# Three batch buffers, loads by head pairs, weights from iteration 13 on, and a feed-forward part with moving weights

## The chip, the cores and the metric

One core of one Trainium2 chip runs the kernel. The metric is the device time of one execution in microseconds (us), as the median of several runs; lower is better.

## What is computed

Two stages. The first is a linear attention with decay, over 4 batches, 8 heads, 768 steps and head size 48; the second a soft mixture of 8 experts over the 3072 rows that the first one makes.

```python
# attention: r, k, v are (4, 8, 768, 48), w and u are (8, 48), all f32
for t in range(S):
    cur = np.einsum('bhd,bhe->bhde', u[None] * kt, vt)
    y[:, :, t] = np.einsum('bhd,bhde->bhe', rt, state + cur)
    state = w[None, :, :, None] * state + np.einsum('bhd,bhe->bhde', kt, vt)
x = y as (3072, 384)                      # rows are (batch, step)
# experts: phi (384, 32), w1 (8, 384, 1024), w2 (8, 1024, 384); 4 slots per expert
logits = x @ phi
d = softmax of logits over the 3072 rows; slot_input = d.T @ x      # (32, 384)
for e in range(E):
    h = np.maximum(slot_input[e] @ w1[e], 0.0)
    slot_out[e] = h @ w2[e]
c = softmax of logits over the 32 slots; out = c @ slot_out         # (3072, 384)
```

## The kernel before, in words

**Units of work.** Two heads make a pair (96 columns), so a batch has 4 pairs and the kernel 16, numbered m. The 768 steps of a pair are two groups g of 3 chunks of 128 steps; an iteration i of the main loop (L420, i from -5 to 31) is one group of one pair, software-pipelined: at iteration i the engines finish group i (`y_pe`), form the masked attention matrix of group i+1 (`a_pe`, `mask_f`), bring v of group i+2 into step order (`v_pe`) and transpose k or r of a later pair (`t_pe`). Everything is emitted in the order of the code and each engine works through its own queue in that order.

**One pair.** GpSimd scales k and r with powers of w (`scale`, L196, into one of three buffers `kr`), from f32 tables W that VectorE multiplies and ScalarE exponentiates, one table for each pair index of a batch (`table`, L164 and L166). TensorE transposes them into the banks T0 and T1 (L203), ScalarE copies them out as kT and rT (L209), TensorE transposes kT back (L215), VectorE copies that out as kn (L220) and multiplies prod (L225). For each group: `a_pe` (L264), 64-row matmuls on the two halves of the array in turn; the mask AT on VectorE (L269), which is used here as the milestone of an iteration; `m_pe` (L279 to L294) for the state; `z_evac` on VectorE (L304 to L310); `y_pe` (L320 to L333); `y_evac` on ScalarE into x (L340).

**Routing.** From iteration 8 on, `route` adds for the groups that are finished: transposes of x (L355), logits (L348), their exponentials Lexp (L369), the sums over rows (`disp`, L386, into the same bank Mb that `m_pe` uses, accumulated in `acc`, L393), and the transposed exponentials LexpT (L375, L379). The last groups are routed after the loop (L466 to L492), up to `uns` (L498), the slots' inputs.

**Loads.** SyncE issues a batch as three DMAs of 1152 KB (k, r, v; L105, L109) into one of two buffers `raw`. Batches 0 and 1 are issued at the start, batch 2 at iteration 2 and batch 3 at iteration 10, into buffers that batches 0 and 1 have used up (L457, L459). w comes as one DMA that writes its row to all 128 partitions (L99), and with u a second time as `wu` from ScalarE's queue (L101, L102) for a transpose (L178) that yields `wuT`, `ucol` and `wT`. GpSimd's queue carries the expert weights, cast from f32 to bf16 on the way: one DMA for each of the 16 matrices, w1 of the 8 experts, then w2, spread over the iterations from -1 to 22 by the table `W_AT` (L418). w2 of the last four experts lies in `raw[0]`.

**Feed-forward and output** (L501 to L548). The weights are the stationary operand: 192 matmuls of 128x128 weights with 4 moving columns for w1 (L507), relu on ScalarE (L510), 24 row sums of LexpT (L512), another 192 for w2 (L522), copies to `soT` (L524), 3 transposes (L527), a copy to `so` (L528). Then 24 matmuls of 384 columns (L542) from six banks, which VectorE and ScalarE in turn scale and copy out (L544, L546), and 7 stores (L548).

## Time and profile before

| what | value |
|---|---|
| median of 3 runs | 164.96 us (164.61 to 164.97) |
| the profiled execution's own time | 164.48 us |
| its span, first to last instruction | 162.7 us |
| mean granted TensorE clock | 0.832 |
| PE, PEld busy | 112.8 us (69%), 92.7 us (57%) |
| DVE (VectorE), ACT (ScalarE), POOL (GpSimd) busy | 97.9 us (60%), 85.0 us (52%), 57.7 us (35%) |
| HBM read, written | 39.57 MB, 4.72 MB |

The profile shows one execution. PE is TensorE's matmuls and PEld its weight loads, which run beside them; SP is SyncE, which here only issues DMAs. A line of a group or a timeline names the source line, the engine, the operation, what it writes and reads (out<-in), the shape and the count. Ahead of an instruction stands in brackets how long its engine had been idle and what released it. The granted clock is the share of full speed at which TensorE was allowed to run. A busy engine need not be what the end waits for: the chain of waits, followed back from the last instruction, shows that.

### The profile page before, as it was taken

The numbers are of one execution on the slowest core, as the hardware profiler recorded it, in microseconds if no ns is written. First come the engines' busy times: TensorE is split into PE (matmuls) and PEld (weight loads), VectorE is DVE, ScalarE is ACT, GpSimd is POOL, SyncE is SP. The second block draws the span as 40 slices with busy tenths as digits, with TensorE's granted clock in tenths as the row PEclk, the third lists the DMA queues.
The fourth block names the chain that finished last, engine by engine and source line by source line (L and its number), as shares of the span: only waits on it lengthen the run. The fifth ranks groups of instructions, "written<-read, shape, count | busy, mean of one in ns | idle before, by whom it ended". The sixth has DMA issues, their size and how long they took to land. (4 is left out here: it accounts for less than half of the span.)

```text
span 162.7 us, 4640 instructions
## 1 busy us (share of the span) xinstructions
PE 112.8 (69%) x1964; PEld 92.7 (57%) x1964; DVE 97.9 (60%) x202; ACT 85.0 (52%) x173; POOL 57.7 (35%) x61
## 2 busy tenths in 40 slices
PE   0023597688889760495997889599597799976840
PEld 0013395476778650385876678487486599962310
DVE  4421589999999951099399469569864300225650
ACT  3413957658777610795576398177355411005550
POOL 5053474799924007996009992000000000000000
PEclk9999999999999998589599699879959755555555
DMA  4999999599999999999999999950000000002996
GB/s 66 314 377 352 385 312 181 115 225 282 225 231 236 232 283 359 376 222 231 223 224 267 210 213 213 214 114 0 6 0 0 4 4 0 4 4 97 387 420 257
DMA packets 21500, 32.00 MB, mean 197 GB/s; under 512 B 1000, under 2 KB 17512, under 8 KB 21480
## 3 DMA queue, kind: packets, MB, share of 16 engines
q0 software_dynamic: 3328, 12.58, 38.9%
q1 hardware_dynamic: 18128, 19.12, 35.6%
q8 instruction: 15, 0.25, 0.6%
q14 instruction: 5, 0.04, 0.1%
q10 hardware_dynamic: 24, 0.00, 0.0%
HBM read 39.57 MB, written 4.72 MB: 272 GB/s over the span
## 5 line engine op out<-in xcount | busy, mean ns | idle before, releaser
L196 POOL TENSOR_TENSOR kr<-raw,W 128x576 bf16<-128x576 f32 x32 | 44.6, 1409 | 34.3 <-DMA raw<-in_r_dram 11.6
L269 DVE TENSOR_TENSOR AT<-Ab,mask_ut 128x768 bf16<-128x768 f32 x32 | 30.4, 951 | 6.5 <-PE Ab L264 6.5
L203 PE MATMUL T<-ident,kr 128*128 128x128 bf16 x192 | 18.6, 242 | 5.7 <-POOL kr L196 5.7
L209 ACT COPY kT<-T 128x768 bf16<-128x768 bf16 x16 | 12.8, 803 | 18.2 <-PE T L203 18.2
L249 PEld LDWEIGHTS <-Q 128*128 128x128 bf16 x288 | 17.7, 106 | 5.4 <-issue 4.2
L249 PE MATMUL Vb<-v_bf,Q 128*128 128x96 bf16 x288 | 19.5, 219 | 1.6 <-ACT v_bf L234 1.6
L220 DVE COPY kn<-T 128x768 bf16<-128x768 bf16 x16 | 8.9, 554 | 14.7 <-PE T L215 14.5
L203 PEld LDWEIGHTS <-kr 128*128 128x128 bf16 x192 | 13.6, 109 | 6.2 <-POOL kr L196 6.2
L225 DVE TENSOR_TENSOR prod<-T,kT 128x768 bf16<-128x768 bf16 x16 | 15.2, 949 | 1.6 <-ACT rT L209 1.6
L340 ACT CAST x<-Yb 128x288 bf16<-128x288 f32 x32 | 12.8, 399 | 5.6 <-PE Yb L333 5.0
L209 ACT COPY rT<-T 128x768 bf16<-128x768 bf16 x16 | 12.8, 799 | 5.0 <-PE T L203 3.4
L310 DVE TENSOR_TENSOR dv<-vn,Mb 128x288 bf16<-128x288 bf16 x32 | 14.2, 445 | 0.0
L234 ACT CAST v_bf<-raw 128x1152 bf16<-128x1152 f32 x8 | 9.2, 1154 | 8.3 <-DMA raw<-in_v_dram 8.3
L255 ACT CAST vn<-Vb 128x288 bf16<-128x288 f32 x32 | 12.9, 402 | 1.1 <-PE Vb L249 0.5
L264 PE MATMUL Ab<-rT,kT 64*128 64x128 bf16 x192 | 11.9, 235 | 1.9 <-DVE AT L269 1.8
L331 PE MATMUL Yb<-Z,rT 128*128 128x96 bf16 x80 | 10.5, 217 | 2.7 <-DVE Z L308 2.7
L290 PE MATMUL Mb<-vn,kn 128*128 128x96 bf16 (+2 forms) x80 | 12.3, 256 | 0.0
L308 DVE TENSOR_TENSOR Z<-Mb,bmask 128x192 bf16<-128x192 f32 x32 | 11.1, 348 | 0.0
L320 PE MATMUL Yb<-vn,AT 128*128 128x48 bf16 x192 | 10.9, 191 | 0.0
L333 PE MATMUL Yb<-dv,ident 128*128 128x288 bf16 x32 | 10.0, 311 | 1.3
L386 PE MATMUL Mb<-Lexp,x 128*128 128x32 bf16 x72 | 3.3, 180 | 9.5 <-DVE dv L310 8.6
L320 PEld LDWEIGHTS <-AT 128*128 128x128 bf16 x192 | 7.4, 100 | 3.7 <-issue 1.0
(119 smaller groups left out, 209.4 us busy)
## 6 DMA issues: line engine op xcount, KB each, us to landing
w_all<-in_moe_w_dram POOLq DMA_DIRECT2D x8, 768.0 KB, 9.7
raw<-in_k_dram SPq DMA_DIRECT2D x4, 1152.0 KB, 12.3
raw<-in_r_dram SPq DMA_DIRECT2D x4, 1152.0 KB, 10.7
raw<-in_v_dram SPq DMA_DIRECT2D x4, 1152.0 KB, 19.9
w_own<-in_moe_w_dram POOLq DMA_DIRECT2D x4, 768.0 KB, 11.2
raw<-in_moe_w_dram POOLq DMA_DIRECT2D x4, 768.0 KB, 13.1
out_dram<-raw SPq DMA_DIRECT2D x3, 768.0 KB, 3.3
out_dram<-W SPq DMA_DIRECT2D x2, 768.0 KB, 3.7
```

The source lines that it names most:

```text
L196: O(pool.tensor_mul(kr[:, j].rearrange("p j (h s) -> p j h s", s=64)[:, :, :, 0:D], src, W[j][:, q].rearrange("p j (h d) -> p j h d", h=2)))
L203: O(pe.transpose(bank[:, x * C:(x + 1) * C], kr[:, j, x, :], ident[:]))
L209: O(act.copy(t[:].rearrange("p (s j) -> p s j", j=J), bank[:, 0:S].rearrange("p (j s) -> p s j", j=J)))
L225: O(dve.tensor_mul(pr[:].rearrange("p (s j) -> p s j", j=J), T1[:, 0:S].rearrange("p (j s) -> p s j", j=J), st["kT", m][:].rearrange("p (s ...
L249: O(pe.matmul(Vb[:, c * P2:(c + 1) * P2], Q3[:, o:o + C], vb[:, 2 * q:2 * q + 2, j, :], start=(j == 0), stop=(j == JV - 1)))
L255: O(act.copy(vn[:].rearrange("p c e d -> p (c e d)"), Vb[:, 0:L * P2]))
L264: O(pe.matmul(Ab[:, e, c * C:(c + 1) * C], kT[s, t], rT[s, t]))
L269: O(dve.tensor_mul(AT[:], Ab[:, :, 0:T].rearrange("p e (c t) -> p e c t", c=L), mask_ut[:, None, None, :].to_broadcast([128, 2, L, C])))
L290: O(pe.matmul(o, kn[:, g * L + c, :], vc, start=first, stop=True, skip_group_check=True))
L310: O(dve.tensor_mul(dv[:], st["v", i][:].rearrange("p c e d -> p (c e) d"), Mb[:, 288:288 + 2 * L, None].to_broadcast([128, L * 2, D])))
L320: O(pe.matmul(Yb[:, o:o + D], AT[:, e, c, :], vn[:, c, e, :], start=first, stop=False, skip_group_check=True))
L340: O(act.copy(st["x", n][:, :, q * P2:(q + 1) * P2], Yb[:, 0:L * P2].rearrange("p (c e) -> p c e", c=L)))
```

## The change

- **Buffers.** Three `raw` buffers instead of two, so batch 2 has its own and its loads follow batches 0 and 1 at once; batch 3 reuses `raw[0]` from iteration 3 on. `w2_own` is gone: w2 of experts 0 to 3 lies in `raw[1]`, of experts 4 to 7 in `raw[2]`, and the output buffers in `raw[0]`.
- **Loads by pairs.** Batches 0 and 1 come in four pieces of two heads, k, r, v each (24 DMAs of a quarter's size); batches 2 and 3 whole. v is cast once a pair (576 columns a partition) instead of once a group of a batch (1152).
- **Weights.** `W_AT` issues them from iteration 13 to 28, the last one after the loop in two halves. w2 is read in longer rows.
- **Start.** w comes as one row to one partition and is spread by an f32 matmul of 384 columns; TensorE gets 5 dummy matmuls of 512 columns ahead of it and 7 before the loop (`keep_warm`). The first pair is scaled by VectorE instead of GpSimd; memsets move from VectorE to GpSimd; the tables are made in the middle of an iteration, one iteration later.
- **Feed-forward.** The slots' inputs are the stationary operand (32 columns, of which the 4 of one expert and zeros), the weights move: 48 matmuls of 512 columns for w1, 64 of 384 for w2. The four experts of a half write to PSUM partitions 0, 32, 64 and 96, that is, to four column strips of the array. h is transposed in between (16 transposes, two copies of 1024). In w2's first half (experts 0 to 3) the four strips alternate; in the second half each expert's 8 matmuls follow one another. Lexp, LexpT and `so` are laid out over 128 partitions for it, with zeros between.
- **Small moves.** `phi_s` is cast in three pieces, at iteration 4; `le_t` and `let_ev` of group 5 stand ahead of the last transposes.

On VectorE at the start, ahead of the loop's first instructions: W_124 and W_125 (before), W_153 and W_154 (after) are the tables for k and r, kr the scaled pair. Before:

```order
L156 CAST ident<-ident_f 128x128 [waits Pool_49]
L164 TENSOR_TENSOR W_124<-w_rep,sk 128x576 [waits Activation_49]
L164 TENSOR_TENSOR W_125<-w_rep,sr 128x576 [waits DVE_49]
L171 MEMSET bmask 128x96
L172 MEMSET bmask 64x48 [waits DVE_49]
L173 MEMSET bmask 64x48
L175 MEMSET ones 128x128
L177 MEMSET ucol 128x4
L180 COPY wuT<-Yb 128x8 [waits PE_49]
L164 TENSOR_TENSOR W_124<-w_rep,sk 128x576
L220 COPY kn<-T_71 128x768 [waits PE_49,Activation_49]
```

After:

```order
L166 CAST ident<-ident_f 128x128 [waits Pool_49]
L175 TENSOR_TENSOR W_153<-LexpT,sk 128x576 [waits Activation_49]
L175 TENSOR_TENSOR W_154<-LexpT,sr 128x576 [waits DVE_49]
L196 COPY wuT<-Mb 128x8 [waits PE_49]
L212 TENSOR_TENSOR kr_138<-raw_67,W_153 128x12x48 [waits DMAHW1_49,Activation_49]
L212 TENSOR_TENSOR kr_138<-raw_67,W_154 128x12x48 [waits DMAHW3_49,Activation_49]
L175 TENSOR_TENSOR W_153<-LexpT,sk 128x576
L236 COPY kn<-T_71 128x768 [waits PE_49,Activation_49]
```

The two scalings of the first pair now stand on VectorE, behind the copy `wuT` that waits for TensorE's transpose of wu; the memsets are gone from there.

On GpSimd, the weights' place: kr is the scaling of a pair, w_all the first layer's weights. Before, behind the third pair's k:

```order
L196 TENSOR_TENSOR kr_116<-raw_67,W_125 128x12x48 [waits Activation_49]
L196 TENSOR_TENSOR kr_117<-raw_67,W_124 128x12x48 [waits Activation_49]
L123 DMA w_all<-in_moe_w_dram 128x3072
L196 TENSOR_TENSOR kr_117<-raw_67,W_125 128x12x48 [waits Activation_49]
L196 TENSOR_TENSOR kr_115<-raw_67,W_124 128x12x48 [waits PE_49,Activation_49,Pool_49]
```

After, behind the tenth pair's k (pair 9, from batch 2 in raw_69):

```order
L212 TENSOR_TENSOR kr_140<-raw_69,W_153 128x12x48 [waits DMAHW4_49,PE_49,Pool_49]
L212 TENSOR_TENSOR kr_140<-raw_69,W_154 128x12x48 [waits DMAHW5_49,PE_49,Pool_49]
L212 TENSOR_TENSOR kr_138<-raw_69,W_153 128x12x48 [waits PE_49,Pool_49]
L129 DMA w_all<-in_moe_w_dram 128x3072
L212 TENSOR_TENSOR kr_138<-raw_69,W_154 128x12x48 [waits PE_49,Pool_49]
```

The first weight load has moved from behind the scaling of pair 2 to behind that of pair 9.

The diff, cut to its core:

```diff
-    raw = [big.tile([128, 3 * RW], f32, name=f"raw{j}") for j in range(2)]
+    NR = 3
+    EG = E // 2
+    raw = [big.tile([128, 3 * RW], f32, name=f"raw{j}") for j in range(NR)]
...
     def w2_of(e):
-        t = w2_own[:, e, :] if e < E - nLate else w2_late[:, (e - E + nLate) * eW2:(e - E + nLate + 1) * eW2]
-        return t.rearrange("p (f d) -> p f d", f=nF)
+        g, j = divmod(e, EG)
+        return raw[1 + g][:].bitcast(bf)[:, j * eW2:(j + 1) * eW2].rearrange("p (y d) -> p y d", y=nF)
...
-    O(sp.dma_start(out=w_rep[:], in_=w.flatten().partition_broadcast(128)))
+    O(sp.dma_start(out=w_row, in_=w.rearrange("(o h) d -> o (h d)", o=1)))
...
+    def load_batch(b, step):
+        for h0 in range(0, H, step):
+            load_kr(0, k, b, h0, h0 + step)
+            load_kr(1, r, b, h0, h0 + step)
+            load_v(b, h0, h0 + step)
+
+    load_batch(0, 2)
+    load_batch(1, 2)
     O(sp.dma_start(out=phi_f[:], in_=moe_phi.rearrange("(mo p) s -> p mo s", p=128)))
+    load_batch(2, H)
...
+    def keep_warm(n, cols=512):
+        for _ in range(n):
+            O(pe.matmul(Yb[:, 0:cols], warm[:, 0:128], warm[:, 0:cols], start=True, stop=True))
...
-    O(act.activation(out=lnw[:], in_=w_rep[:], func=AF.Ln))
+    keep_warm(5)
+    O(pe.matmul(Xb[:, 0:H * D], one_f, w_row, start=True, stop=True))
+    O(act.activation(out=lnw, in_=Xb[:, 0:H * D], func=AF.Ln))
...
+        eng = dve if m == 0 else pool
+        O(eng.tensor_mul(kr[:, j].rearrange("p j (h s) -> p j h s", s=64)[:, :, :, 0:D], src,
...
-    W_AT = {-1: 1, 1: 1, 3: 1, 5: 1, 7: 1, 9: 1, 11: 1, 13: 1, 15: 1, 17: 1, 19: 1, 20: 1, 21: 2, 22: 2}
+    W_AT = {13: 1, 14: 1, 15: 1, 17: 1, 18: 1, 20: 1, 21: 1, 23: 1, 24: 1, 26: 1, 27: 3, 28: 2}
     nw = 0
+    keep_warm(7)
...
+        j, q = (i + 5) % 2, (i + 5) // 2
+        if 1 <= q < nQ:
+            table(j, q)
         if odd and 0 <= mu + 3 < nU:
             scale(mu + 3, 0)
...
+        if odd and 0 <= mu + 2 < nU:
+            v_cast(mu + 2)
...
-        if i == 2:
-            O(dve.tensor_copy(phi_s[:], phi_f[:]))
-            load_batch(2)
-        if i == 10:
-            load_batch(3)
+        if i == 3:
+            load_batch(3, H)
+        if i == 4:
+            for mi in range(nM):
+                O(dve.tensor_copy(phi_s[:, mi, :].rearrange("p (j g s) -> p g j s", g=2, s=Spe),
+                                  phi_f[:, mi, :].rearrange("p (g j s) -> p g j s", g=2, s=Spe)))
...
+    for g in range(2):
+        for a in range(2):
             for mi in range(nM):
+                for j in range(EG):
+                    O(pe.matmul(hb[g][a][32 * j:32 * j + 32, 0:FH], uns[:, mi, g, j, :],
+                                w1_all[:, g * EG + j, mi, a * FH:(a + 1) * FH],
+                                start=(mi == 0), stop=(mi == nM - 1), skip_group_check=True))
+            src = hb[g][a][:, 0:FH].rearrange("p (q y) -> p y q", y=nF)
+            dst = h_sb[g][:, :, a * PH:(a + 1) * PH]
+            if a == 0:
+                O(act.activation(out=dst, in_=src, func=AF.Relu))
+            else:
+                O(dve.tensor_scalar(out=dst, in0=src, scalar1=0.0, scalar2=None, op0=ALU.max))
     for i in range(nN):
...
+    for g in range(2):
+        bank = (T0, T1)[g]
+        for y in range(nF):
+            O(pe.transpose(bank[:, y * C:(y + 1) * C], h_sb[g][:, y, :], ident[:]))
+        O(dve.tensor_copy(hT[g].rearrange("p y c -> p (y c)"), bank[:]))
+    SO = Mb[:, 0:Dm]
+
+    def w2_mm(g, j, y):
+        O(pe.matmul(SO[32 * j:32 * j + 32, :], hT[g][:, y, 32 * j:32 * j + 32], w2_of(g * EG + j)[:, y, :],
+                    start=(g == 0 and y == 0), stop=(g == 1 and y == nF - 1), skip_group_check=True))
+
+    for y in range(nF):
+        for j in range(EG):
+            w2_mm(0, j, y)
+    for j in range(EG):
+        for y in range(nF):
+            w2_mm(1, j, y)
+    so = cst.tile([128, Dm], bf, name="so")
+    O(dve.tensor_copy(so[:, 0:Dm // 2], SO[:, 0:Dm // 2]))
+    O(act.copy(so[:, Dm // 2:Dm], SO[:, Dm // 2:Dm]))
...
-    ob = [T1[:].bitcast(f32), Ab[:, 0, :], Ab[:, 1, :], Mb[:], Yb[:], Xb[:]]
+    ob = [T1[:].bitcast(f32), Ab[:, 0, :], Ab[:, 1, :], T0[:].bitcast(f32), Yb[:], Xb[:]]
```

151 lines of the change are left out of this document (67 added, 84 removed).

## The prediction

> **What bounds the kernel now.** I read the page first, then the stage windows, VectorE's timeline, the waits and the chain. In the windows the columns are length, then busy time and instruction count of PE, PEld, DVE, ACT and POOL, the granted TensorE clock, DMA share and GB/s.
>
> ```profile
> 40.75:55.37 14.62, 13.31 (x257) 11.19 (x256) 13.99 (x28) 11.32 (x23) 6.92 (x7) 1.00 1.04 231
> 59.54:69.93 10.39, 3.60 (x55) 3.07 (x55) 2.38 (x6) 4.18 (x8) 8.04 (x7) 0.70 1.10 353
> 77.50:80.90 3.40, 3.40 (x48) 2.68 (x45) 1.25 (x2) 1.61 (x4) 0.00 (x0) 0.53 1.08 221
> 80.90:91.10 10.20, 8.22 (x164) 7.03 (x161) 8.78 (x18) 6.22 (x14) 5.65 (x6) 0.99 1.08 238
> 96.00:104.00 8.00, 5.68 (x121) 5.00 (x120) 7.50 (x14) 5.81 (x13) 2.75 (x3) 1.00 1.08 213
> 128.70:146.07 17.37, 15.21 (x418) 14.57 (x416) 2.85 (x13) 2.42 (x10) 0.00 (x0) 0.50 0.01 3
> 146.07:158.00 11.93, 8.44 (x24) 3.62 (x23) 7.31 (x12) 6.97 (x12) 0.00 (x0) 0.50 0.71 286
> ```
>
> The loop is VectorE's where nothing else holds it: 13.99 of 14.62 us busy from one mask AT to the sixth after it, so 2.4 us an iteration. Between 59.54 and 69.93 VectorE is busy 2.38 of 10.39 us. The last two rows are the feed-forward part and the output: TensorE at half clock throughout. VectorE's timeline gives the milestones (start, length, instruction, idle before and releaser):
>
> ```profile
> 20.44 0.96 DVE L269 TENSOR_TENSOR AT<-Ab,mask_ut 128x768 bf16<-128x768 f32 x1 [0.56 <-PE Ab L264]
> 59.54 0.96 DVE L269 TENSOR_TENSOR AT<-Ab,mask_ut 128x768 bf16<-128x768 f32 x1 [0.87 <-PE Ab L264]
> 61.85 2.75 POOL L196 TENSOR_TENSOR kr<-raw,W 128x576 bf16<-128x576 f32 x2 [10.43 <-DMA raw<-in_r_dram]
> 69.93 0.95 DVE L269 TENSOR_TENSOR AT<-Ab,mask_ut 128x768 bf16<-128x768 f32 x1
> 79.73 0.96 DVE L269 TENSOR_TENSOR AT<-Ab,mask_ut 128x768 bf16<-128x768 f32 x1 [1.66 <-PE Ab L264]
> 82.87 0.95 DVE L269 TENSOR_TENSOR AT<-Ab,mask_ut 128x768 bf16<-128x768 f32 x1
> 121.20 0.96 DVE L269 TENSOR_TENSOR AT<-Ab,mask_ut 128x768 bf16<-128x768 f32 x1
> 129.34 0.26 DVE L498 TENSOR_TENSOR uns<-acc,csr 128x96 bf16<-128x96 f32 x1
> ```
>
> So the span is five stages: start to the first mask at 20.44, loop to the last at 121.20 with one hole (GpSimd, and behind it everyone, waits for r of batch 2), routing of the last groups to 129.6, feed-forward to 146.07, output to 162.7.
>
> **Start.** The chain to the first mask:
>
> ```profile
> 8.34 0.24 PE L178 MATMUL Yb<-ident_f,wu 8*128 8x8 f32 x1 [8.34 <-DMA wu<-in_u_dram]
> 8.62 0.17 DVE L180 COPY wuT<-Yb 128x8 f32<-128x8 f32 x1 [0.65 <-PE Yb L178]
> 6.53 0.75 DVE L164 TENSOR_TENSOR W<-w_rep,sr 128x576 f32<-128x576 f32 x1
> 11.32 0.82 PE L203 MATMUL T<-ident,kr 128*128 128x128 bf16 x6 [2.74 <-POOL kr L196]
> 15.80 1.15 ACT L234 CAST v_bf<-raw 128x1152 bf16<-128x1152 f32 x1 [2.82 <-DMA raw<-in_v_dram]
> 16.86 0.68 ACT L166 ACTIVATE W<-W 128x576 f32<-128x576 f32 x1
> 17.44 0.78 ACT L209 COPY rT<-T 128x768 bf16<-128x768 bf16 x1
> 17.00 0.88 PE L249 MATMUL Vb<-v_bf,Q 128*128 128x96 bf16 x9 [1.64 <-ACT v_bf L234]
> 19.82 0.50 PE L264 MATMUL Ab<-rT,kT 64*128 64x128 bf16 x6
> 110.53 0.50 PE L203 MATMUL T<-ident,kr 128*128 128x128 bf16 x6
> 110.96 0.34 PE L264 MATMUL Ab<-rT,kT 64*128 64x128 bf16 x6
> ```
>
> Loads by pairs take the wait for v (15.80) away: a first pair is a quarter of a batch. What is late next is wu, which nothing in the change speeds directly: its copy still stands in VectorE's queue, now ahead of the first scaling (two multiplications, priced at the table row's 0.75 us each), and in TensorE's queue seven 512-column dummies stand behind its transpose. With wu as late as now: transpose over at 8.6, scaling over at 9.6, dummies over at 11.6 at half clock (0.43 us each, from 0.32 us for 384 columns, quoted below) or at 10.1 at full clock. From there: transposes 0.82, kT 0.8, exp 0.68, rT 0.78, the pair's v cast 0.68 (576 elements, like the exp), v matmuls 0.88, next transposes 0.82, a-matmuls 0.50 and some eight handovers of 0.05: 6.4 us, or 5.2 us at full clock (0.50 and 0.34 in the 110 us rows, v in proportion). First mask at 18.0 or 15.3. Were wu in by 5 us, the tables (second multiplication over at 7.3, then exp) would set 13.3. The five early dummies may or may not leave the clock up across the wait for wu, so I take the middle, 16.3: **-4.1 us** (-2.4 to -7.1). Spreading w by TensorE instead of a 128-fold DMA counts for nothing: its dummies, then an f32 matmul of 384 columns, end about when the broadcast landed (5.3 us, since the first multiplication waits for it and starts at 5.85).
>
> **Loop.** VectorE also gets one table multiplication more behind the first mask, four instead of three (+0.75), and three small casts of phi in place of this one:
>
> ```profile
> L456 DVE CAST phi_s<-phi_f 128x96 bf16<-128x96 f32 x1 | 1.4, 1412 | 0.0
> L220 DVE COPY kn<-T 128x768 bf16<-128x768 bf16 x16 | 8.9, 554 | 14.7 <-PE T L215 14.5
> L196 POOL TENSOR_TENSOR kr<-raw,W 128x576 bf16<-128x576 f32 x32 | 44.6, 1409 | 34.3 <-DMA raw<-in_r_dram 11.6 <-PE Yb L331 9.7 <-ACT W L166 6.3
> ```
>
> The cast takes as long as one GpSimd scaling (1412 against 1409 ns) though it is eight times smaller than kn's copy at 554: it probably stood against GpSimd. Three casts cost 0.3 us each if they don't, 1.4 each if they do: 0.9 to 4.2 against 1.4; I take 0.9, nearer to the copy's rate. Sum **+0.2** (+0.2 to +3.5). ScalarE casts v once a pair instead of eight times a kernel: 16 x 0.68 for 8 x 1.15, 1.7 us more on an engine that is busy 11.32 of 14.62 us, hidden unless it delays the v matmuls by more than the gap they have; nothing counted, 2 us at most.
>
> The hole goes. With a third buffer the loads of batch 2 follow the first two without waiting for a buffer. A batch is three loads of 1152 KB, and weights no longer share the engines with them:
>
> ```profile
> GB/s 66 314 377 352 385 312 181 115 225 282 225 231 236 232 283 359 376 222 231 223 224 267 210 213 213 214 114 0 6 0 0 4 4 0 4 4 97 387 420 257
> q0 software_dynamic: 3328, 12.58, 38.9%
> raw<-in_r_dram SPq DMA_DIRECT2D x4, 1152.0 KB, 10.7
> ```
>
> In the slices from 8 to 20 us, 4.07 us each, the loads run at 352 to 385 GB/s; at 370 a batch takes 9.6 us. Three are in by 35 us, the fourth (issued once batch 0 is used up, near 30 us) by 45, and GpSimd asks for batch 2 at about 38, for batch 3 past 50. The step from the mask at 59.54 to the next then costs 3.1 us, as from 79.73 to 82.87, not 10.4: **-7.25**. The cover for this is the later weights: 12.58 MB at 213 GB/s (the window from 96) take 59 us. GpSimd reaches the first weight behind the first scaling of pair 9, whose buffer is free once pair 6 is transposed, near the tenth mask at 45 us; so they are in by 106, and the feed-forward part now begins at about 118. Without that slack of 12 us, each us of late weights would be a us of time.
>
> **Feed-forward.** Row by row from the chain of waits:
>
> ```profile
> 129.65 0.93 PE Vb L507 x24
> 130.58 0.81 PE Ab L507 x24
> 131.42 0.21 ACT hT L510
> 137.02 1.77 PE Mb L512 x24
> 148.05 0.32 PE Mb L542
> ```
>
> Now 384 small matmuls, 24 row sums, transposes: 129.65 to 146.07, 16.4 us. The changed part streams weights instead: 48 matmuls of 512 columns, 64 of 384, each 32 columns of the array wide. At half clock 384 columns take 0.32 us, 1200 a us; at full clock twice that (six transposes: 0.82 against 0.50). Where four strips run at once a quarter counts. The trace has no column strips, but it has row strips: six matmuls on alternating halves (L264) take 0.34 us where six on the whole array take 0.50, that is, they start in pairs. So the first layer streams 6144 columns, the second 3072 for experts 0 to 3 and 32 x 384 = 12288 for experts 4 to 7, which the code takes one expert after the other: those stay in one strip and overlap nothing. Beside these: the second half of experts 0-3 waits for ScalarE's relu on the shared tile Ab (0.7, as at 131.42 now), row sums 1.8 (1.2), eight transposes 0.85 (0.45), a 1024-wide copy 0.75 (from 0.55 for 768; the second hides behind experts 0-3), final copies 0.4. Half clock throughout: 5.1+0.7+1.8+0.85+0.75+2.6+10.2+0.4 = 22.4. Full throughout: 2.7+0.7+1.2+0.45+0.75+1.3+5.4+0.4 = 12.9. In the loop a half-clock stretch ends after 3.4 us of busy TensorE (77.50 to 80.90, then 0.99). With 3.4 us of that in the first layer and 4 in the second, behind the row sums and copies: 4.3+0.7+1.5+0.65+0.75+8.6+0.4 = 16.9, **+0.5** (-3.5 to +6.0). A second `uns` multiplication adds **+0.3**.
>
> The Trainium skill (TensorE: Matmul & The Clock Gate, Part 3: Packing small matmuls) gives a measured 2.38 times for three column strips, not 3. By that share the overlapped 9216 columns would cost a quarter more: 1 to 2 us, an estimate from that page, and the time 1 to 2 us above my sum. No row here shows column strips, so the sum stays with the row strips.
>
> **Output.** Evacuations, sizes and the six banks' order stay. At full clock the first 2-tile store leaves some 0.4 us earlier, and TensorE (8.44 of 11.93 us) no longer paces the stores:
>
> ```profile
> 147.55 0.36 SPq L548 DMA_DIRECT2D out_dram<-raw  x1
> 157.88 0.33 SPq L548 DMA_DIRECT2D out_dram<-raw  x1
> HBM read 39.57 MB, written 4.72 MB: 272 GB/s over the span
> ```
>
> 4.72 MB at the 420 GB/s of the best slice above are 11.2 us where the stores now spread over some 13.8: **-1.3** (0 to -2.9).
>
> **Sum.** -4.1 +0.2 -7.25 +0.5 +0.3 -1.3 = -11.65 from the profiled execution's 164.48 (span 162.7): 152.8. That run was 0.5 below the median, 164.96; against the median I say **153.3 us**.
>
> **Rivals.** (1) The clock stays at half from the feed-forward part on. For it: it does so now for 30 us, though TensorE is busy 8.44 of 11.93 us in the output stage. Against it: those matmuls use 32 of 128 rows or 4 columns; the new ones stream 128 rows without a break. Feed-forward +6.0, output 0: -4.85, 160.1. The Trainium skill (TensorE: Matmul & The Clock Gate, Part 1: The HAM clock gate) has the clock back after one busy window of about 3.4 us and knows only half and full, which speaks against this rival. The loop's 77.50 row agrees with that; the last two rows of the first fence, 30 us of mostly busy TensorE at half clock, do not. (2) The clock is full from the first dummies and never falls: start 15.3, feed-forward -3.5: -16.65, 148.3. (3) Slower: column strips don't overlap. Then 24576 columns stream in each layer. At the tail's present clock that is 20.5+0.7+1.8+0.85+0.75+20.5+0.4 = 45.5, +29.1, and with the other terms 183; with the clock recovering, 12.4 and 12.6 for the layers, 29.0 in all, +12.6: 165.4. It decides from the point where the feed-forward part takes 28 us. Against it: the row strips' pairs.
>
> **Chances.** Forecast 0.50 (its own range 150 to 157), rival 1 0.20, rival 2 0.20, rival 3 0.10, of which 0.06 slower, 0.02 same, 0.02 faster when the rest gains more. Within 0.3%, half a us, a measurement tells no change. So faster 0.92, same 0.02, slower 0.06. The range takes in rivals 1 and 2 with some 1.5 us beyond each, for the bounds of the start and of phi: 146.5 to 161.5; rival 3 is left out.
>
> **What would show it.** First mask between 13 and 18 us; no wait of GpSimd for `raw` over 1 us after the start; last mask near 110, `uns` near 118; feed-forward matmuls starting in fours, 3 to 10 ns apart, and 13 to 22 us from `uns` to the first output matmul; the granted clock above 0.5 in the second layer. I am wrong if strips start 0.2 us apart or more, if the mask cadence rises over 2.5 us where VectorE was full, or if VectorE waits for weights' or v's casts.

## The result

The changed kernel takes 150.06 us (median of 4 runs, 148.27 to 152.28) where the kernel before takes 164.79 on the same chip: ratio 0.9036, 95% interval 0.8968 to 0.9104. The forecast was 153.3 us, 146.5 to 161.5. The ratio and its interval, here and below, leave out the slow runs, those over 1.5% above the quickest of the same kernel, and so lie under the ratio of the medians. Runs of the changed kernel lie further apart than those of the kernel before: in its traces TensorE's granted clock falls to half for stretches of 3.41 us or a multiple, and the mean clock of the four runs goes from 0.897 to 0.947, highest in the quickest. So stages are compared below, and the half-clock stretches in them counted. The trace of the changed kernel is of its quickest run, 148.27 us, and shows the least half clock of the four.

The changed kernel's windows by stage (length, then busy time and count of PE, PEld, DVE, ACT and POOL, granted clock, DMA share, GB/s): first to fourteenth mask, to the 19th, to the last, to `uns`, to the first output matmul, to the end.

```profile
15.19:55.82 40.63, 30.76 (x534) 25.57 (x533) 36.40 (x67) 27.16 (x54) 27.46 (x22) 0.92 0.85 264
55.82:71.59 15.77, 12.09 (x242) 10.17 (x240) 12.47 (x25) 10.20 (x24) 8.08 (x9) 1.00 1.01 200
71.59:108.72 37.13, 30.75 (x612) 25.95 (x612) 31.02 (x62) 27.61 (x62) 14.15 (x17) 1.00 1.01 196
108.72:116.95 8.23, 5.28 (x112) 4.38 (x114) 4.19 (x13) 4.42 (x12) 0.00 (x0) 1.00 0.83 166
116.95:130.42 13.47, 11.59 (x153) 7.11 (x154) 3.34 (x7) 1.51 (x3) 0.00 (x0) 0.87 0.01 1
130.42:146.50 16.08, 5.18 (x24) 3.42 (x23) 6.76 (x12) 6.21 (x12) 0.00 (x0) 0.84 0.72 293
```

Against the same stages of before:

| stage | before | after | difference | forecast |
|---|---|---|---|---|
| start to first mask | 20.44 | 15.19 | -5.25 | -4.1 |
| masks 1 to 14 | 34.93 | 40.63 | **+5.70** | +0.2 |
| masks 14 to 19 (the hole) | 24.36 | 15.77 | -8.59 | -7.25 |
| masks 19 to 32 | 41.47 | 37.13 | **-4.34** | 0 |
| last mask to `uns` | 8.40 | 8.23 | -0.17 | +0.3 |
| `uns` to first output matmul | 16.47 | 13.47 | **-3.00** | +0.5 |
| output | 16.63 | 16.08 | -0.55 | -1.3 |
| span | 162.7 | 146.5 | -16.2 | -11.65 |

The total was inside the range, but the three terms in bold were wrong by 3.5 to 5.5 us and partly cancelled. All of the +5.70 lies ahead of the eighth mask (20.3 us before, 26.0 after); masks 8 to 14 took 14.62 us in both kernels. VectorE's timeline shows the hole gone (before, the step from the mask at 59.54 took 10.39 us) and phi's casts, which took 1.41 us as one:

```profile
15.19 0.96 DVE L285 TENSOR_TENSOR AT<-Ab,mask_ut 128x768 bf16<-128x768 f32 x1 [0.24 <-PE Ab L280]
...
36.11 2.99 DVE L477 CAST phi_s<-phi_f 128x32 bf16<-128x32 f32 x3
...
59.79 0.96 DVE L285 TENSOR_TENSOR AT<-Ab,mask_ut 128x768 bf16<-128x768 f32 x1 [0.67 <-PE Ab L280]
...
62.80 0.95 DVE L285 TENSOR_TENSOR AT<-Ab,mask_ut 128x768 bf16<-128x768 f32 x1
```

What held the kernel before in the hole is not only GpSimd's wait for r of batch 2. That ended at 61.85, and the scaled r was ready at 63.2. ScalarE waited for v of the same batch until 65.5, and behind the cast of v in its queue stood the copies of xT, which TensorE needed first (ScalarE's and TensorE's timelines of the kernel before):

```profile
65.53 1.15 ACT L234 CAST v_bf<-raw 128x1152 bf16<-128x1152 f32 x1 [5.47 <-DMA raw<-in_v_dram]
...
67.48 0.26 PE L348 MATMUL Xb<-phi_s,xT 128*128 128x32 bf16 x3 [6.79 <-ACT xT L364]
```

The transposes of that r came behind, at 67.86. In the changed kernel all three loads of batch 2 are in early, and v's cast also stands later: it is reached 6.8 us behind the fourteenth mask (62.61), before 4.7 us behind it (60.06).

GpSimd, which waited 10.43 us for r of batch 2, now waits more in the first iterations for the tables, and TensorE behind it for `kr`. The groups (busy, mean ns, idle before and its releasers):

```profile
L212 POOL TENSOR_TENSOR kr<-raw,W 128x576 bf16<-128x576 f32 x30 | 41.9, 1412 | 31.1 <-PE T L219 15.2 <-ACT W L177 9.5 <-issue 3.7
L265 PE MATMUL Vb<-v_bf,Q 128*128 128x96 bf16 x288 | 18.1, 210 | 7.3 <-ACT v_bf L250 7.3
L219 PE MATMUL T<-ident,kr 128*128 128x128 bf16 x192 | 16.8, 228 | 4.3 <-POOL kr L212 4.3
```

The waits for `T` (15.2) are GpSimd running ahead of its buffers. The 9.5 us for `W` are four waits, the longest 3.4, all behind the first mask; the kernel before had 6.3 us of them, but 4.7 ahead of its first mask. Of the feed-forward part, TensorE's timeline:

```profile
116.89 1.09 PE L535 MATMUL Ab<-w_all,uns 128*32 128x512 bf16 x12 [0.73 <-DVE uns L519]
118.73 1.47 PE L535 MATMUL Ab<-w_all,uns 128*32 128x512 bf16 x12 [0.75 <-ACT W L541]
119.96 1.22 PE L535 MATMUL Vb<-w_all,uns 128*32 128x512 bf16 x12
121.00 0.83 PE L535 MATMUL Yb<-w_all,uns 128*32 128x512 bf16 x12
121.76 1.84 PE L545 MATMUL Xb<-ones,LexpT 128*128 128x1 bf16 x24
123.46 1.05 PE L552 MATMUL T<-ident,W 128*128 128x128 bf16 x16
124.85 4.77 PE L557 MATMUL Mb<-raw,W 128*32 128x384 bf16 x64 [0.34 <-DVE W L553]
```

Twelve matmuls of 512 columns in 0.83 us: four strips do run at once (at full clock the trace has them starting within 17 ns of each other, the next four 0.216 us later). The clock over the span's 40 slices, and what the DMAs moved, from the page:

```profile
PEclk9999559999999999999999999999999959999975
...
GB/s 96 337 372 375 370 364 376 382 327 386 368 145 2 20 190 215 214 183 214 175 174 158 184 200 172 216 215 214 215 216 206 104 0 4 0 0 269 415 416 190
```

In this execution the clock was at half from 14.9 to 21.8, from 117.3 to 120.7 and from 141.2 on, nowhere in between. Its records begin at 11.5 us; a 9 ahead of that is no record, and the dummies there ran at half speed (seven of 512 columns in 3.17 us). The kernel before has records from 22.7 us on; it lost the clock again and again between masks 19 and 32, and for good from 128.5 on:

```profile
79.73:121.20 41.47, 35.05 (x607) 29.55 (x607) 31.12 (x61) 26.84 (x58) 13.29 (x12) 0.87 0.74 152
```

A mean of 0.87 over 41.47 us is 10.8 us at half (2 x 0.13 x 41.47). The output now writes at 415 GB/s, which suggests that the transfers, not TensorE, set its end.

### The profile page after: what moved, and what is told of

The parts are those of the page before. It is cut to its first block, busy times and chain, and to the rows that moved or that the text cites. A ratio compares the mean times of both kernels' runs of the same rounds, so it can differ in the third digit from the quotient of the medians.

```text
span 146.5 us, 4187 instructions
## 1 busy us (share of the span) xinstructions
PE 105.9 (72%) x1719; PEld 81.6 (56%) x1719; DVE 101.9 (70%) x200; ACT 83.8 (57%) x176; POOL 56.5 (39%) x68
## 5 line engine op out<-in xcount | busy, mean ns | idle before, releaser
L212 POOL TENSOR_TENSOR kr<-raw,W 128x576 bf16<-128x576 f32 x30 | 41.9, 1412 | 31.1 <-PE T L219 15.2
L285 DVE TENSOR_TENSOR AT<-Ab,mask_ut 128x768 bf16<-128x768 f32 x32 | 30.4, 951 | 3.3 <-PE Ab L280 3.3
L265 PE MATMUL Vb<-v_bf,Q 128*128 128x96 bf16 x288 | 18.1, 210 | 7.3 <-ACT v_bf L250 7.3
L265 PEld LDWEIGHTS <-Q 128*128 128x128 bf16 x288 | 16.2, 100 | 11.5 <-issue 11.0
L219 PE MATMUL T<-ident,kr 128*128 128x128 bf16 x192 | 16.8, 228 | 4.3 <-POOL kr L212 4.3
L219 PEld LDWEIGHTS <-kr 128*128 128x128 bf16 x192 | 12.5, 103 | 5.1 <-POOL kr L212 4.6
L241 DVE TENSOR_TENSOR prod<-T,kT 128x768 bf16<-128x768 bf16 x16 | 15.2, 948 | 0.1
L280 PE MATMUL Ab<-rT,kT 64*128 64x128 bf16 x192 | 11.1, 222 | 2.2 <-DVE AT L285 2.1
L250 ACT CAST v_bf<-raw 128x576 bf16<-128x576 f32 x16 | 10.8, 675 | 0.0
L349 PE MATMUL Yb<-dv,ident 128*128 128x288 bf16 x32 | 9.2, 289 | 0.6
L347 PE MATMUL Yb<-Z,rT 128*128 128x96 bf16 x80 | 8.9, 205 | 0.5 <-DVE Z L324 0.5
L380 ACT COPY xT<-Xb 128x384 bf16<-128x384 bf16 x18 | 8.8, 486 | 0.3 <-PE Xb L371 0.2
```

The lines of the kernel that those rows point to most:

```text
L212: O(eng.tensor_mul(kr[:, j].rearrange("p j (h s) -> p j h s", s=64)[:, :, :, 0:D], src, W[j][:, q].rearrange("p j (h d) -> p j h d", h=2)))
L219: O(pe.transpose(bank[:, x * C:(x + 1) * C], kr[:, j, x, :], ident[:]))
L241: O(dve.tensor_mul(pr[:].rearrange("p (s j) -> p s j", j=J), T1[:, 0:S].rearrange("p (j s) -> p s j", j=J), st["kT", m][:].rearrange("p (s ...
L265: O(pe.matmul(Vb[:, c * P2:(c + 1) * P2], Q3[:, o:o + C], vb[:, :, g, j, :], start=(j == 0), stop=(j == JV - 1)))
L280: O(pe.matmul(Ab[:, e, c * C:(c + 1) * C], kT[s, t], rT[s, t]))
L285: O(dve.tensor_mul(AT[:], Ab[:, :, 0:T].rearrange("p e (c t) -> p e c t", c=L), mask_ut[:, None, None, :].to_broadcast([128, 2, L, C])))
```

## The experiments

Each is the changed kernel with the edit shown.

**Tables at their old place.**

```diff
-        j, q = (i + 5) % 2, (i + 5) // 2      # ahead of the scalings of iteration i
-        if 1 <= q < nQ:
-            table(j, q)
...
         route(i, 1)
+        q, j = divmod(i + 6, 2)
+        if 1 <= q < nQ:
+            table(j, q)
```

> The changed kernel with the tables' exponentials at the end of the iteration before, as in the kernel before, and nothing else. Theory A (the 5.7 us lost between the first and the fourteenth mask come mostly from tables that are made in the same iteration just ahead of the scaling that needs them: GpSimd waits 9.5 us for W, TensorE behind it 4.3 us for kr): first mask at 15 to 16, GpSimd's wait for W under 3 us, first to fourteenth mask 36.5 to 37.5 instead of 40.63, time about 3.5 us under the changed kernel's. Rival B (the half-clock stretch from 15.2 to 22.0 and v's casts by pairs set the pace there): the wait for W turns into another and first to fourteenth mask stays at 40 to 41.

Measured: first to eighth mask 22.61 us instead of 26.02, with the clock at half in the same place (14.6 to 21.5); first to fourteenth 37.65 instead of 40.63, with one half-clock stretch more in it (38.5 to 41.9). The first mask comes 0.94 later; one more table multiplication now stands directly ahead of it on VectorE. The time, 148.39 us (147.02 to 151.64; 0.9007 of before, 0.8944 to 0.9071), cannot be told from the changed kernel's (0.8968 to 0.9104); the feed-forward part of its profiled execution met more half clock (16.19 us against 13.47). The group of GpSimd's scalings, and VectorE at the first mask:

```profile
L212 POOL TENSOR_TENSOR kr<-raw,W 128x576 bf16<-128x576 f32 x30 | 42.5, 1430 | 28.6 <-PE T L219 16.6 <-ACT W L177 5.3 <-issue 4.7
```

```profile
15.46 0.74 DVE L175 TENSOR_TENSOR W<-LexpT,sk 128x576 f32<-128x576 f32 x1
16.13 0.94 DVE L285 TENSOR_TENSOR AT<-Ab,mask_ut 128x768 bf16<-128x768 f32 x1
```

The wait for `W` fell from 9.5 to 5.3 (not under 3), TensorE's for `kr` from 4.3 to 0.4, and the stage by 3.0 to 3.4 us. Theory A holds for that much; rival B expected no change. Five other kernels below with this part of the loop untouched took 25.8 to 27.6 us from the first to the eighth mask, with 3.4 to 13.5 us of half clock in it, so the 3.4 us are clear of that spread.

**Phi's casts on ScalarE**, with three more of the same shape on VectorE late in the loop, into a tile that nobody reads.

```diff
-                O(dve.tensor_copy(phi_s[:, mi, :]..., phi_f[:, mi, :]...))
+                O(act.copy(phi_s[:, mi, :]..., phi_f[:, mi, :]...))
+        if i == 28:
+            for mi in range(nM):
+                O(dve.tensor_copy(phi_q[:, mi, :]..., phi_f[:, mi, :]...))
```

> The changed kernel with phi's three casts on ScalarE instead of VectorE at the same place; three casts of the same shape into a tile that nobody reads are added on VectorE in iteration 28, when GpSimd scales nothing any more. Theory A (the casts took 1.0 us each because they stood against GpSimd's back-to-back scalings): the added casts take 0.2 to 0.4 us each, and first to fourteenth mask falls by about 2 us, from 40.63 to 38.5, since VectorE sets the pace at that place. Rival B (such a cast with its strided columns is slow by itself): the added casts take about 1.0 us each. Rival C (VectorE is not what the loop waits for there): first to fourteenth mask stays within 0.5 of 40.63.

Measured: first to fourteenth mask 38.57, 2.06 less, although one more half-clock stretch (31.1 to 34.5) lay in it; time 148.50 us (0.8955, 0.889 to 0.9021), which again cannot be told from the changed kernel's. The casts, by group:

```profile
L482 DVE CAST phi_q<-phi_f 128x32 bf16<-128x32 f32 x3 | 0.3, 175 | 0.0
L478 ACT CAST phi_s<-phi_f 128x32 bf16<-128x32 f32 x3 | 0.5, 219 | 0.0
```

On VectorE the same cast takes 175 ns when GpSimd scales nothing, against 1051 ns (2.99 for three) beside its scalings; ScalarE does it in 219 ns at 36 us, in the middle of those scalings. Theory A holds, and VectorE was what that place waited for.

**The second layer's second half in fours.**

```diff
-    for j in range(EG):
-        for y in range(nF):
+    for y in range(nF):
+        for j in range(EG):
             w2_mm(1, j, y)
```

> The changed kernel with the second layer's second half (experts 4 to 7) taken four strips at a time, like its first half. Theory A (four strips run at once: 0.1625 us a step of four): those 32 matmuls take 1.3 us instead of 3.3, the time falls by 2.0 us. Rival B (strips that follow one another overlap whatever their order, and the array or the moving data's path is the bound): 3.0 to 3.3 us as now and no change in the time. The prediction's own price, one expert after the other without overlap, would have been 5.4 us.

Measured: the second half's starts span 1.59 us (131.55 to 133.14) against 3.13 in the changed kernel, with some 0.9 us of it at half clock; time 147.66 us, 0.8863 (0.883 to 0.8895), below the changed kernel's interval. The combined and kept busy kernel below, at full clock, shows the layer without that:

```profile
118.44 2.78 PE L565 MATMUL Mb<-raw,W 128*32 128x384 bf16 x64 [0.34 <-DVE W L561]
```

4.77 to 2.78 is the 2.0 us of theory A. The prediction's own price was wrong too: taken one expert after the other, the 32 matmuls were not serial (that would be 5.1 us), but overlapped in pairs. The trace has an expert's last four starting 5 to 17 ns from the next one's first four.

**v's cast an iteration earlier**, with a third buffer.

```diff
-        if odd and 0 <= mu + 2 < nU:        # behind the transposes
+        if not odd and 0 <= mu + 2 < nU:    # ahead of them, one iteration earlier
             v_cast(mu + 2)
```

> The changed kernel with v's cast of a pair one iteration earlier (even iteration, three buffers). Rival B of the tables' run (v's casts by pairs hold the loop up: TensorE waits 7.3 us for v_bf in 15 places): first to fourteenth mask falls by 2 to 3 us, the routing part of the loop (mask 18 to 31) by 1 to 2 us. Theory A (those waits lie beside VectorE's work or behind the tables): TensorE's wait for v_bf goes and the stages stay within 0.7 us, the gap turning up as a wait for something else.

Measured: 152.98 us (152.12 to 154.71; 0.9297, 0.9256 to 0.9338), no gain. TensorE's wait for the cast is gone, and others stand in its place:

```profile
L212 POOL TENSOR_TENSOR kr<-raw,W 128x576 bf16<-128x576 f32 x30 | 41.8, 1404 | 31.3 <-PE T L219 15.9 <-ACT W L177 7.9 <-issue 5.8
L265 PE MATMUL Vb<-v_bf,Q 128*128 128x96 bf16 x288 | 19.0, 215 | 0.0
L219 PE MATMUL T<-ident,kr 128*128 128x128 bf16 x192 | 17.5, 234 | 7.5 <-POOL kr L212 7.5
```

First to fourteenth mask took 39.75 us, with one half-clock stretch in it where the changed kernel has two. Masks 19 to 32 took 40.23 with nearly three (70.2 to 73.6, 94.1 to 97.5, 107.8 to the last mask), 3.1 us more than with none, that is, the 1.0 to 1.1 a stretch that other kernels pay below. The feed-forward part, whose code is the same, took 16.40 us with more half clock. So the casts by pairs do not hold the loop up, and the longer time lies in the stages that met half clock; whether the earlier cast brings on more of it was not tried.

**What took the hole away**: three kernels. In the first, batch 2 goes into batch 0's buffer as before (its load stands behind the last use of batch 0), the weights stay late; w2's places and the output buffers move with it. In the second, the third buffer stays and the first layer's weights go out early, as before, and the second layer's follow from iteration 18 on. The third has both undone.

```diff
-        return raw[b % NR][:, which * RW:(which + 1) * RW]
+        return raw[(0, 1, 0, 2)[b]][:, which * RW:(which + 1) * RW]
```

```diff
-    W_AT = {13: 1, 14: 1, 15: 1, 17: 1, ...}
+    W_AT = {-1: 1, 1: 1, 3: 1, 5: 1, 7: 1, 9: 1, 11: 1, 13: 1, 18: 1, ...}
```

> The changed kernel with batch 2 loaded into batch 0's buffer once that is used up, as in the kernel before (batch 3 goes into the third buffer); the weights stay late. Theory A (the third buffer is what took the hole away): GpSimd waits for raw of batch 2 as before, 5 us or more, and the masks 14 to 19 take 20 us or more instead of 15.77. Rival B (the late weights alone take it away): batch 2's three loads are issued at about 28, 32 and 34 us, as batch 3's are now, take 9.6 us together at 370 GB/s with nothing beside them, and are in by 40 to 43, when GpSimd first asks for them (its scaling of pair 8 began at 43.1 us): 15.77 stays within 0.7, the time within the run-to-run spread of the changed kernel.

> The changed kernel with the first layer's eight weights issued from iteration -1 to 13, as in the kernel before, and the third buffer kept. Theory A (late weights are needed: the prediction named them as the cover): weights and loads share the bandwidth again, GpSimd waits for raw of batch 2 or 3, masks 14 to 19 take 18 us or more. Rival B (the third buffer alone takes the hole away, since its loads are issued by 25 us): no wait for raw over 1 us, 15.77 stays within 0.7; the issues on GpSimd (0.6 us each) may cost up to 1 us between the first and the fourteenth mask.

> The changed kernel with both undone: batch 2 in batch 0's buffer and the first layer's weights early. If each of the two alone is enough (rival B of both runs), only here does the hole come back: GpSimd waits 4 to 10 us for raw of batch 2, masks 8 to 19 take 4 to 7 us more than in the changed kernel (30.4 there), the time 154 to 157. If the loads by pairs at the start, which leave the queue earlier, were what counted, there would be no hole here either.

Measured: 153.48 us (0.9313, 0.922 to 0.9405), 157.02 (0.9561, 0.9438 to 0.9683) and 159.44. Masks 14 to 19 took 15.78, 16.56 and 15.78: no hole at that place in any. In the trace r of batch 2 is in at 30.4 us in the changed kernel, at 39.0 and 40.7 with one part undone, and at 59.7 with both; in the kernel before it released GpSimd at 61.85. GpSimd asks for it at 45 in the changed kernel. The first is still slower than the changed kernel by the ratios; in its trace masks 14 to 32 take as long, and the longer parts are masks 1 to 14 (42.18 us) and the feed-forward part (16.16), where it met more half clock. With one part undone the traces have no wait for `raw` behind the start, so either part alone is enough, rival B twice: the late weights because nothing shares the bandwidth, the third buffer because k and r of batch 2 are issued by 23.2 us, when one weight has gone out. v comes only at 63.7 there, still ahead of its cast at 67.0.

With both undone GpSimd's wait did come back. Its timeline in that kernel, the scaling of r of pair 8, the first of batch 2:

```profile
59.82 2.78 POOL L211 TENSOR_TENSOR kr<-raw,W 128x576 bf16<-128x576 f32 x2 [10.48 <-PE T L218]
```

The profile puts the wait down to TensorE's transposes, but those that free this buffer, of pair 5, were over at 49.9; r of batch 2 landed at 59.65. That is a wait of nearly 10 us for the load, as expected. It cost the masks nothing: they need this r only at 66.3, because the loop was late itself, with its fourteenth mask at 60.71, 4.9 us behind the changed kernel's. v landed at 63.3, and its cast stood at 67.5. An estimate for a loop in time, from the changed kernel's rows: r would be needed at 61.4 and is scaled by 61.2, v's cast would be reached at 62.6, so the wait would be some 0.7 us and not 7. So the later place of v's cast, which no run undoes alone, covers a part of what the hole was. No run brings the hole back in the masks (8 to 19 took 31.1 us, not the 34 to 37 expected): what took it away is shown by the landing times and the waits. The wait that did cost time came one batch later. ScalarE's timeline of that kernel, the cast for pair 12:

```profile
95.28 0.67 ACT L249 CAST v_bf<-raw 128x576 bf16<-128x576 f32 x1 [4.06 <-DMA raw<-in_v_dram]
```

Masks 19 to 32 took 43.98, 3.75 more than in the kernel of v's earlier cast, which like this one has nearly three half-clock stretches there. The late loop, and the 157.02 of the second kernel, led to something else. First to eighth mask took 30.81 in the second kernel against 26.02, and VectorE shows where:

```profile
36.07 7.45 DVE L477 CAST phi_s<-phi_f 128x32 bf16<-128x32 f32 x3
43.43 0.94 DVE L285 TENSOR_TENSOR AT<-Ab,mask_ut 128x768 bf16<-128x768 f32 x1
```

Three casts of 0.18 us took 7.45. GpSimd's timeline in the same kernel beside them:

```profile
37.30 2.78 POOL L212 TENSOR_TENSOR kr<-raw,W 128x576 bf16<-128x576 f32 x2
40.01 0.59 POOL L129 DMA_DIRECT2D w_all<-in_moe_w_dram  x1
40.62 2.76 POOL L212 TENSOR_TENSOR kr<-raw,W 128x576 bf16<-128x576 f32 x2
43.33 0.59 POOL L129 DMA_DIRECT2D w_all<-in_moe_w_dram  x1
```

All three end at 43.4 to 43.5, just after GpSimd stops computing to issue a weight. But the first of them had been waiting since 36.07 (it lasts 7.35 us alone), past two such pauses of 0.55 us; why it got in only at the third stays open. In the changed kernel, where nothing is issued there, the casts end 0.09 us after the starts of GpSimd's scalings, one at each. The 4.5 us that the casts take longer are nearly all of the 4.8 that early weights cost in this stage, which also has one more half-clock stretch. The Trainium skill (SBUF — State Buffer, Who interferes with whom) says that VectorE and GpSimd share one port pair under an exclusive lock, that a cast may take it, and that the loser blocks for the whole instruction. The changed kernel agrees: two of its three casts take 1.45 us, as long as one scaling. The 7.35 us here are longer than any one GpSimd instruction, which that rule does not explain.

**No dummies at the start.**

```diff
-    keep_warm(5)
...
-    keep_warm(7)
```

> The changed kernel without the twelve dummy matmuls at the start. Theory A (the seven dummies hold the first transposes up by 2 us: the scaling of k is over at 8.3, the transposes start at 10.3; the full clock that they bring from 11.8 to 14.9 is worth 1.2 us on the chain to the mask): first mask at 13.7 to 14.4 instead of 15.19. Rival B (without them TensorE runs at half clock until the loop is dense, which costs more than the wait): first mask at 15.2 or later, or first to eighth mask longer than 26.0 by over 1 us.

Measured: first mask at 14.32, first to eighth 25.81. The first mask alone proves little, since wu lands at another time in each execution and moves it: kernels with the same start have it between 14.15 and 15.42. Counted from the transpose of wu, which stands in the timeline below, it comes 7.99 us later in the changed kernel, 7.9 to 8.3 in the nine traces with dummies and the tables of the changed kernel, and 6.80 without dummies, 6.8 in all three such kernels. So the dummies cost 1.2 us: theory A. The time, 151.15 us (145.35 to 151.98), is not distinguishable. The transpose of wu, the dummies and the transposes of the first pair in the changed kernel, then the same without dummies, from TensorE's timelines:

```profile
7.20 0.24 PE L194 MATMUL Mb<-ident_f,wu 8*128 8x8 f32 x1 [1.99 <-DVE W L175]
7.38 3.17 PE L137 MATMUL Yb<-LexpT 128*128 128x512 bf16 x7
10.34 1.40 PE L219 MATMUL T<-ident,kr 128*128 128x128 bf16 x12
```

```profile
7.52 0.24 PE L193 MATMUL Mb<-ident_f,wu 8*128 8x8 f32 x1 [3.50 <-DMA wu<-in_u_dram]
8.70 1.49 PE L218 MATMUL T<-ident,kr 128*128 128x128 bf16 x12 [0.94 <-DVE kr L211]
```

wu came 0.3 us later in the second run, and its mask was still 0.9 earlier.

**The old feed-forward in the changed kernel**: 384 small matmuls with the weights stationary.

```diff
-                    O(pe.matmul(hb[g][a][32 * j:32 * j + 32, 0:FH], uns[:, mi, g, j, :],
-                                w1_all[:, g * EG + j, mi, a * FH:(a + 1) * FH], ...))
+                O(pe.matmul(hp[:, fo, :], w1_all[:, e, mi, fo:F:nF],
+                            uns[:, mi, g, j, g * Spe:(g + 1) * Spe], ...))
...
```

The second layer is put back in the same way.

> The changed kernel with the feed-forward computed as in the kernel before (small matmuls, weights stationary, 4 or so columns moving, 8 transposes fewer), everything else as changed. Theory A (the streaming in strips is the gain: 4 strips at once): from uns to the first output matmul 16 to 17 us at half clock as before, against 13.5 to 16.2 in the runs of the changed kernel with 3.4 to 10 us of half clock in it, and its granted clock stays at half to the end. Rival B (the clock alone is the gain, which recovers now because the loop leaves it full): 11 to 13 us, no slower than the changed kernel.

> The kernel of the run before it with the old feed-forward once more, with the weights' rows and columns laid as in the kernel before: every fourth column of w1 goes into a weight load, not every eighth. In that run a weight load of every eighth column took 170 ns against 118 in the kernel before, and 24 of those matmuls 1.58 us against 0.94. If that is the whole excess, 24 take 0.94 us again and uns to the first output matmul 16.3 to 16.5 at half clock, as in the kernel before (16.4): the streaming in strips is then the whole gain of the feed-forward part, clock included. If the rest of the changed kernel slows it, 18 or more; if the clock recovers, 13 or less.

Measured: 158.50 us (0.9523, 0.9494 to 0.9551) with every eighth column in a weight load, 153.09 (0.9312, 0.9269 to 0.9356) with every fourth, as in the kernel before. From `uns` to the first output matmul 21.47 and 16.40 us. The second kernel's windows of that part and of the output, and its weight loads:

```profile
119.55:135.95 16.40, 14.28 (x411) 13.83 (x411) 1.92 (x10) 1.90 (x9) 0.00 (x0) 0.53 0.01 3
135.95:153.00 17.05, 6.56 (x24) 3.57 (x23) 6.94 (x12) 6.42 (x12) 0.00 (x0) 0.70 0.68 277
```

```profile
L535 PEld LDWEIGHTS <-w_all 128*128 128x128 bf16 x192 | 6.7, 118 | 1.5 <-issue 1.5
```

The first kernel has 170 ns there: the excess of 5.1 us was my layout. The old form takes 16.4 us in the changed kernel as it did before, at half clock from 1.2 us behind its start to its end, although the clock was full when it began. The new form does not always take 13.47. In the eight traces that hold it unchanged it takes 12.24 us with no half clock (early weights), 13.47 with 3.4 us of it, and 15.5 to 16.4 with 9 to 10 us; but in each of them the clock was full again before the output began, in neither of the old form's. So theory A stands in part: streaming in strips brings the clock back, and saves 4.2 us where the clock is full all through, under 1 us where it is half for 9 to 10 us. The output part takes 16.0 us behind the new form and 17.0 behind the old.

**Combined**: tables one iteration earlier from the fourth on (the third right behind the first mask), phi on ScalarE, no dummies, both halves of the second layer in fours, the first layer's halves in banks of different tiles. **Combined and kept busy**: the same with dummy matmuls where TensorE waits, from iteration 8 on.

```diff
+        for _ in range(n):
+            O(pe.matmul(Vb[:, 288:512], ident[:], Q3[:, 0:224], start=True, stop=True, ...))
...
+            if i >= LAG and i % 2 == 0:
+                keep_busy(2)
             v_pe(i + 2)
...
+                keep_busy(5)
                 disp(n - 1, False)
```

> The changed kernel with what the runs so far point to: tables one iteration earlier from the fourth on (the third right behind the first mask), phi's casts on ScalarE, no dummies, the second layer's second half in fours, and the first layer's two halves in banks of different tiles. By the single runs: first mask 14.3 (-0.9), first to fourteenth mask 35 to 36 (-3.4 tables, -2 phi), second layer -2, the wait for the relu on Ab -0.7: about 8.5 us under the changed kernel at the same clock, time 140 to 143. If VectorE's order or the clock takes some back: 143 to 147.

> The combined kernel with dummy matmuls of 224 columns at the places where TensorE waits from mask 8 on: two ahead of the v matmuls of every other iteration, five ahead of a group's dispatch, some 20 in the last groups' routing. Theory A (each half-clock stretch follows a stretch in which TensorE was too idle; one costs 1.08 us in the loop, up to 3 us around the feed-forward part): the stretches between mask 18 and the output go, masks 19 to 32 take 37.1 in every run, uns to the first output matmul 9.5 to 11, the runs spread by under 1%, time 2 to 4 us under the combined kernel. Rival B (the stretches come whatever TensorE does, or the dummies cost what they bring): the same number of stretches, or the same time within 1 us.

Measured: 142.42 us (139.87 to 145.70), 0.8585 of before (0.8537 to 0.8632), and 139.73 us (139.07 to 142.03), 0.850 (0.847 to 0.8529). The windows of masks 19 to 32 in the first:

```profile
66.75:106.66 39.91, 33.92 (x607) 28.59 (x607) 31.03 (x62) 27.69 (x62) 13.99 (x17) 0.88 0.98 194
```

and, for the second, masks 1 to 14, 19 to 32, and the feed-forward part:

```profile
13.76:51.42 37.66, 32.58 (x539) 27.10 (x538) 33.54 (x63) 27.03 (x56) 27.98 (x22) 0.91 0.98 301
...
67.15:104.22 37.07, 33.77 (x639) 28.56 (x639) 31.05 (x62) 27.61 (x62) 14.17 (x17) 1.00 1.00 196
...
112.74:122.04 9.30, 8.15 (x152) 5.44 (x153) 3.34 (x6) 1.51 (x3) 0.00 (x0) 1.00 0.02 4
```

With the dummies TensorE is busy 91% of masks 19 to 32 and no half-clock stretch is left between the early loop and the output; the feed-forward part is down to 9.30. Five of its six runs lie within 1% of each other, the sixth at 142.03. Theory A of that run holds. The gain over the combined kernel is 2.7 us between the medians and 1.4 by the ratios, where 2 to 4 were expected. What neither kernel reaches is the sum of the single gains in the early loop: masks 1 to 14 take 37.1 and 37.7 us, not 35 to 36. Each has two half-clock stretches there where the kernel before, with 34.93, has none on record; that these are the rest was not tried.

Over the profiled executions, masks 19 to 32 take 37.1 us with no half-clock stretch (the changed kernel, tables, batch 2 shared, combined and kept busy), 39.1 to 39.3 with two (phi, fours, no dummies) and 40.23 with nearly three (v's cast earlier): 1.0 to 1.1 us a stretch. The one kernel with a single stretch, the old feed-forward's second, pays 1.35. In the kernel before, 10.8 us of half clock, some three stretches, go with 4.34 us more, 1.4 each. Step by step from mask to mask, those that no stretch touches are the same there to 0.04 us, but for one of 3.84 against 3.64, so the clock is nearly all of the difference.

When a stretch comes can be read from the traces. In one execution all changes of the clock lie on a grid of 3.41 us. Twenty drops follow a step of that grid inside this stage, over all fourteen traces; in nineteen of those steps TensorE was busy 50 to 55%, in one 41%. The steps at full clock in this stage without a drop behind them have 56% or more, and 79% or more in the kernel kept busy. From phi's kernel, the step ahead of a drop and the one behind it:

```profile
75.50:78.91 3.41, 1.86 (x37) 1.38 (x35) 3.25 (x7) 2.13 (x5) 1.99 (x3) 1.00 0.88 159
78.92:82.33 3.41, 3.41 (x49) 2.93 (x49) 1.24 (x2) 1.70 (x4) 1.40 (x1) 0.50 1.02 183
```

Such a step holds one of the loop's waits of 1.2 us (1.7 in the kernel before), and the dummies cut these waits to 0.3 us. So whether such a wait costs a stretch seems to depend on where the grid lies against the loop, which differs from trace to trace.

## Why the prediction came out

**Right in size, with the lesser of two waits named:** the hole (10.39 to 3.01 us, -7.4 against -7.25; 1.0 of the stage's other 1.2 us lies in the step from 74.75 to 79.73, which a half-clock stretch of the kernel before meets, 77.3 to 80.7). The prediction had "GpSimd, and behind it everyone, waits for r of batch 2". By the rows, r alone would have held its transposes from about 61.1 to 63.2 us; v, through ScalarE's queue, held them to 67.86. Both are loads of batch 2, so the same cure met both, and the later cast of v helped, which the prediction did not count here. The cover was misjudged too: the prediction named late weights as what the third buffer needs, and the runs show that either does it alone.

**Right in kind, small in size:** the start. wu came in earlier than the 8.34 that was assumed (transposed at 7.20), which is 1.1 of the 1.15 us. From there to the first mask it took 7.99 us, and the forecast's 16.3 has 7.96. That is partly luck: 16.3 was called the middle of 18.0 and 15.3, which is 16.65, and it was chosen between two clocks, not worked out. The dummies cost 1.2 us, as their place in the queue said, and bring nothing for the first mask.

**Wrong: the loop's +0.2.** The step that failed is "VectorE also gets one table multiplication more ... (+0.75)": it priced the moved table by VectorE's time alone and left out who waits for its end. The move from the end of one iteration to the middle of the next put multiplication and exponential directly ahead of the scaling that reads them; undone, the stage gives 3.0 to 3.4 us back. The other part is phi: the prediction saw that the old cast "probably stood against GpSimd", had 4.2 as the bound, and chose 0.9 by the nearer-looking row. 2.99 was measured, and moving it gives 2.1 us. The row to go by was the one with the same conflict. The single gains do not add up: with both mended at once the stage falls by 3.0 to 3.5 us, to 37.1 and 37.7, with two half-clock stretches in it as in the changed kernel. The 2.2 to 2.7 us that are left over 34.93 are about the size of two stretches at the prices above; that they are these two is not shown.

**Wrong: the 0 for masks 19 to 32.** The prediction had no term for the clock in the loop, though the trace of before showed a half-clock row in the loop (77.50 to 80.90). Some three such stretches were 4.3 us of the time before; in the profiled execution of the changed kernel there were none, in those of nearly the same program none to three. This gain is therefore partly chance, as is the 4 us between the runs.

**Wrong: the feed-forward's +0.5.** The mis-sized term is the second layer: 8.6 us forecast, 4.77 measured. About half of that is the order: strips that follow one another overlap in pairs, where the forecast had them serial. The other half is the clock, full there by chance where the forecast had 4 us of half; in six other traces with the same feed-forward code and 9 to 10 us of half clock the whole part took 15.5 to 16.4 us, near the forecast's 16.9. The first layer, with 4.9 us to the row sums, was forecast at 5.0. Rivals 1 and 3 fall: the granted clock is 1.00 from 120.7 to 141.2, and four strips take the time of one. Rival 2 (148.3) is nearest to the profiled execution in its number, not in its reason: the clock did fall, for 6.8 us in the loop and 3.4 in the feed-forward part.

**Wrong in size: the output's -1.3.** It became -0.55: the last store is issued 9.2 us after the first output matmul instead of 11.8, but the transfers, at 415 GB/s in the page's row, are late instead, and the part takes 16.0 us in every kernel with the new feed-forward, whatever its clock.

So the total was right by luck in good part: +5.5 in the loop met -4.3 and -3.5 that were not forecast, and much of the last two is the clock of one execution.

## What to carry to other kernels

Price a moved instruction by who waits for its end, not only by the engine it runs on. Where two engines wait for loads of one batch, follow the wait that ended last: a long wait need not be the one that holds the rest. Keep small VectorE casts out of stretches where GpSimd computes back to back: a 0.18 us cast costs a whole GpSimd instruction, or several. Count the stretches of half clock in both traces before giving a stage's gain to an edit; where TensorE waits a little in every iteration, dummies in those waits are worth trying (1.4 to 2.7 us here). Count a time from the event that released it when that event itself comes at another time in each run, as wu does.
